# A sliding-window attention followed by a sentence-level mixture of experts: row sums and normalisation in another layout, and the two stages interleaved

**Chip, cores, metric.** One core of a Trainium2 chip. The metric is the device time of one execution in microseconds (us); most executions of a kernel here agree within about 1%.

## The reference

```python
def _attn_ref(q, k, v):                       # (8 batches, 8 heads, 576, 64)
    scores = q @ k.T / sqrt(64)               # per batch and head
    mask = (rel >= 0) & (rel < 64)            # causal, window 64
    attn = softmax(where(mask, scores, -1e9))
    return attn @ v

def _moe_ref(x, w_gate, w1, w2):              # x: (8, 576, 512)
    logits = x.mean(axis=1) @ w_gate          # one expert per batch ("sentence")
    e = argmax(logits); g = softmax(logits)[e]
    return g * (relu(x @ w1[e]) @ w2[e])      # w1[e]: 512 x 1024, w2[e]: 1024 x 512
```

A batch's expert depends on the mean of its whole attention output, so its weights (4 MB of fp32) can be asked for only when its attention is done. Nothing in one batch depends on another.

## The kernel before

It has three stages one after the other: attention of all batches, one gate for all, the MLP of all batches. Attention works on a head pair of a batch at a time (32 pairs), with queries along the free dimension. The row sums come from a second set of matmuls with a matrix of ones, so each sum lies 64 times, once per output row, and the reciprocal runs over all 576 columns:

```python
def stage_b(prev):
    avp = ps_a.tile([128, 1024], FP32, tag="avp")
    lbp = ps_a.tile([128, 1024], FP32, tag="lbp")
    for (j, qlo, qhi, st, sp) in segs:
        for (lhs, op) in ((pvt, avp), (None, lbp)):      # V, then ones
            for hh in range(2):
                ...                                      # 64x64 tiles of the array
    nc.scalar.copy(out=avs, in_=avp[:, 0:S])
    nc.scalar.copy(out=lbs, in_=lbp[:, 0:S])
    nc.vector.reciprocal(out=rl, in_=lbs)                # 128 x 576, L128
    nc.vector.tensor_tensor_reduce(out=xT[:, pbb, php, :], in0=avs, in1=rl, ...)
...
for bb in range(B):                                      # the MLP, after everything
    ...                                                  # load w1t, w2t of the batch's expert
    for ft in range(8):
        php = ps_h.tile([128, 2, 512], FP32, tag="php")  # two banks, bufs=2
        ...                                              # 8 matmuls of 288 columns, relu
    for mt in range(NST):
        ...                                              # 8 matmuls of 512 columns, copy, DMA out
```

The softmax here doesn't subtract the row's maximum and nothing guards it: scores larger than these inputs give would overflow.

## Time and profile before

| | before |
|---|---|
| time, median of 15 runs | 359.7 us (357.2 to 360.9) |
| attention, up to the start of the gate | about 204 us |
| gate and wait for the first expert weights | about 12 us |
| MLP of eight batches, TensorE without a gap | 136 us |
| VectorE's reciprocals | 32 x 3.75 = 119.9 us |

In the lines below, PE is TensorE, PEld its weight loads, DVE is VectorE, ACT is ScalarE, POOL is GpSimd and SPq the queue of SyncE. "Busy" of an engine is the time in which it works on an instruction. "PEclk" is TensorE's granted clock as a share of full speed. In a group line the two numbers after the bar are the group's total busy time and the mean of one instruction in ns, and after the next bar comes the engine's idle time just before, with what ended it. The "pitch" of matmuls is the time from the start of one to the start of the next. The lines of the kernel before are in the prediction.

### The profile page before, as it was taken

Reading aid. Unit: us, or ns where it says so; the run is one execution under the profiler, and the core shown is the slowest. Engines: PE = TensorE matmul, PEld = TensorE weight load, DVE = VectorE, ACT = ScalarE, POOL = GpSimd, SP = SyncE. Lnnn points to the kernel's source line nnn. Section 1 sums busy time; section 2 is a strip of 40 time slices with the busy share of each in tenths; the row PEclk is TensorE's granted clock in tenths of the full one; section 3 lists DMA queues with packets and bytes.
Section 4 is the critical chain, followed back from the end, with each engine's and each line's share of the span. In section 5 each row is a group of like instructions: output and inputs, shape, how many; then the busy total and the mean of one; then the engine's idle time right before and its main releaser. Section 6 shows DMA issues by size and latency. Waiting matters only on the chain.

```text
span 356.7 us, 7472 instructions
## 1 busy us (share of the span) xinstructions
PE 281.1 (79%) x3018; PEld 194.7 (55%) x3018; DVE 189.8 (53%) x179; ACT 185.1 (52%) x356; POOL 130.9 (37%) x189
## 2 busy tenths in 40 slices
PE   0587687778787777787884207999999999999995
PEld 0365565656565665665674205565747474756562
DVE  0049997888887978888879910212130303030312
ACT  2578867676867676767676103342415060605140
POOL 9978665656565656566500030000000011000000
PEclk9999855655655556556556556999999999999999
DMA  9999999999999999999700049999999999998303
GB/s 119 172 153 153 139 125 91 116 96 118 96 118 92 116 99 116 99 112 100 70 3 2 0 77 198 209 266 175 226 164 238 162 229 182 197 221 145 132 29 105
DMA packets 141234, 46.91 MB, mean 132 GB/s; under 512 B 124304, under 2 KB 132496, under 8 KB 141200
## 3 DMA queue, kind: packets, MB, share of 16 engines
q0 software_dynamic: 96416, 27.26, 78.4%
q1 hardware_dynamic: 44784, 19.18, 22.3%
q8 instruction: 24, 0.39, 0.5%
q14 instruction: 10, 0.08, 0.1%
HBM read 63.95 MB, written 9.44 MB: 206 GB/s over the span
## 4 chain that ended last, share of the span: by engine, by line
PE 69%; ACT 17%; issue 5%; DVE 4%; DMA 4%; POOL 1%; POOLq 0%; ACTq 0%; DVEq 0%
PE pso L257 20%; PE php L245 19%; PE tp L171 9%; ACT pt L101 8%; PE lbp L116 8%; PE sps L94 7%; PE avp L116 5%; ACT qT L175 5%; DMA w1t<-in_moe_w_dram 2%; DVE rl L128 2%; ACT kT L175 2%; PE tp L176 2%; DMA qn<-in_q_dram 2%; ACT qT L180 1%; DVE xT L129 1%
## 5 line engine op out<-in xcount | busy, mean ns | idle before, releaser
L128 DVE RECIPROCAL rl<-lbs 128x576 f32<-128x576 f32 x32 | 119.9, 3750 | 24.3 <-ACT lbs L127 24.3
L249 ACT ACTIVATE hT<-php,gwb 128x576 f16<-128x576 f32 x64 | 47.4, 740 | 90.2 <-PE php L245 90.2
L261 DVE COPY ob<-pso 128x512 f32<-128x512 f32 (+1 forms) x40 | 27.6, 689 | 117.3 <-PE pso L257 103.4
L245 PE MATMUL php<-xT,w1t 128*128 128x288 f16 x512 | 66.6, 290 | 8.3 <-DMA w1t<-in_moe_w_dram 8.3
L257 PE MATMUL pso<-w2t,hT 128*128 128x512 f16 (+1 forms) x320 | 71.3, 380 | 0.0
L116 PE MATMUL avp<-pt,vt 64*64 64x128 f16 (+1 forms) x640 | 68.5, 272 | 1.4 <-DVE pt L103 1.4
L116 PE MATMUL lbp<-pt,ones 64*64 64x128 f16 (+1 forms) x640 | 68.7, 271 | 0.0
L116 PEld LDWEIGHTS <-vt 64*64 64x64 f16 x640 | 53.0, 147 | 24.9 <-issue 20.2
L245 PEld LDWEIGHTS <-w1t 128*128 128x128 f16 x512 | 50.0, 99 | 25.4 <-issue 11.2
L156 POOL DMA_DIRECT2D qn<-in_q_dram x63 | 55.0, 876 | 23.5 <-PE tp L176 22.5
L156 POOL DMA_DIRECT2D kn<-in_k_dram x63 | 54.8, 872 | 18.2 <-PE tp L176 17.4
L116 PEld LDWEIGHTS <-ones 64*64 64x64 f16 x640 | 54.6, 150 | 7.6 <-issue 5.7
L257 PEld LDWEIGHTS <-hT 128*128 128x128 f16 (+1 forms) x320 | 31.4, 100 | 37.2 <-issue 3.4
L238 POOL DMA_DIRECT2D w1t<-in_moe_w_dram x8 | 6.0, 756 | 78.1 <-PE php L245 50.5
L101 ACT ACTIVATE pt<-sps 128x1024 f16<-128x1024 f32 x32 | 33.5, 1045 | 0.8 <-PE sps L94 0.8
L94 PEld LDWEIGHTS <-kT 64*64 64x64 bf16 x576 | 27.1, 151 | 9.8 <-issue 9.3
L103 DVE TENSOR_TENSOR pt<-pt,bandm 128x1152 f16<-128x1152 f16 x32 | 22.4, 701 | 18.7 <-ACT pt L102 18.7
L94 PE MATMUL sps<-qT,kT 64*64 64x128 bf16 x512 | 32.2, 289 | 0.0
L126 ACT COPY avs<-avp 128x576 f32<-128x576 f32 x32 | 20.5, 642 | 21.7 <-PE lbp L116 21.1
L171 PE MATMUL tp<-ident,kn 128*128 128x128 bf16 x128 | 16.9, 276 | 15.0 <-ACT qT L180 14.8
L175 ACT CAST kT<-tp 128x512 bf16<-128x512 f32 x32 | 18.8, 588 | 16.4 <-PE tp L171 16.4
L171 PE MATMUL tp<-ident,qn 128*128 128x128 bf16 x128 | 18.6, 297 | 9.8 <-DMA qn<-in_q_dram 9.8
(49 smaller groups left out, 188.2 us busy)
## 6 DMA issues: line engine op xcount, KB each, us to landing
vn<-in_v_dram SPq DMA_DIRECT2D x64, 144.0 KB, 3.3
w1t<-in_moe_w_dram POOLq DMA_DIRECT2D x8, 1024.0 KB, 10.1
w2t<-in_moe_w_dram POOLq DMA_DIRECT2D x8, 1024.0 KB, 10.3
out_dram<-ob SPq DMA_DIRECT2D x32, 256.0 KB, 5.9
qn<-in_q_dram POOLq DMA_DIRECT2D x63, 80.0 KB, 3.6
kn<-in_k_dram POOLq DMA_DIRECT2D x63, 80.0 KB, 3.3
out_dram<-ob SPq DMA_DIRECT2D x8, 128.0 KB, 6.2
bandm<-bandm SPq DMA_DIRECT2D x1, 256.0 KB, 4.6
```

What stands on the lines that cost most here:

```text
L94: nc.tensor.matmul(out=sdst[p0:p0 + 64, :], lhsT=pkT[p0:p0 + 64, ts(j, 64)], rhs=pqT[p0:p0 + 64, j * 64:j * 64 + 128], start=True, stop=Tr ...
L101: nc.scalar.activation(out=pt[:, 0:8, :], in_=sps, func=AF.Exp, scale=scale)
L103: nc.vector.tensor_tensor(out=pt, in0=pt, in1=bandm, op=ALU.mult)
L116: nc.tensor.matmul(out=op[p0:p0 + 64, qlo:qhi], lhsT=lh, rhs=ppt[p0:p0 + 64, j, qlo - 64 * j:qhi - 64 * j], start=st, stop=sp, tile_positi ...
L128: nc.vector.reciprocal(out=rl, in_=lbs)
L156: nc.gpsimd.dma_start(out=tl[:, :, hh, :], in_=tf[hidx:hidx + 640].rearrange("(st p) d -> p st d", p=128))
L171: nc.tensor.matmul(out=tp[:, ts(st, 128)], lhsT=tl[:, st].rearrange("p h d -> p (h d)"), rhs=ident, start=True, stop=True)
L175: nc.scalar.copy(out=dst[:, 0:512], in_=tp)
L245: nc.tensor.matmul(out=php[:, sc, 0:SC], lhsT=w1t[:, kb, ts(ft, 128)], rhs=xT[:, bb, kb, ts(sc, SC)], start=(kb == 0), stop=(kb == 3))
L249: nc.scalar.activation(out=hT[:, ft].rearrange("p (sc s) -> p sc s", sc=2), in_=php[:, :, 0:SC], func=AF.Relu, scale=gwb[:, bb:bb + 1])
L257: nc.tensor.matmul(out=pso[0:n], lhsT=hT[:, fb, mt * 128:mt * 128 + n], rhs=w2t[:, fb, :], start=(fb == 0), stop=(fb == 7))
L261: nc.vector.tensor_copy(out=ob[0:n], in_=pso[0:n])
```

## The change

Its intent: make the reciprocal small, take attention's waits off TensorE by running the MLP of batch b-2 beside the attention of batch b, and move Q and K in larger rows. The diff replaces most of the kernel; its core:

```diff
-            nc.scalar.copy(out=avs, in_=avp[:, 0:S])
-            nc.scalar.copy(out=lbs, in_=lbp[:, 0:S])
-            nc.vector.reciprocal(out=rl, in_=lbs)
-            nc.vector.tensor_tensor_reduce(out=xT[:, pbb, php, :], in0=avs, in1=rl, ...)
+    def st_s(u):        # scores of one slot (128 queries, 8 heads): matmuls, exp, mask product
+    def st_a(u):        # product with [V | 1]; queries on the partitions
+        for h in range(H):
+            for jj in range(nj):
+                nc.tensor.matmul(out=av[64*jj:64*jj+64, h//4, c:c+D+1],
+                    lhsT=pt[:, h%2, h//2, jj, :], rhs=vx[:, 1-jj, i, h, :], ...)
+        nc.vector.reciprocal(out=rl[0:n], in_=avv[0:n, :, :, D:D + 1])        # 8 elements
+        for a in range(2):
+            nc.vector.tensor_tensor(out=x[0:n, a], in0=avv[0:n, a, :, 0:D],
+                                    in1=rl[0:n, a].broadcast_to([n, 4, D]), op=ALU.mult)
+    def st_x(u):        # transpose x back, copy it, row sums for the gate
+    def cast_v(b):      # V to fp16: one copy on VectorE, two (shifted by 64 rows) on GpSimd
+    def gate(b):        # one batch's expert, and its weight DMAs
+    def moe_chunks(b):  # 16 chunks of 4 relu matmuls (one bank, ps_m bufs=2), then 5 of 8
... (loads of Q and K as 2 KB source rows, transposes through PSUM, masks)
+        for s in range(NSLOT + 4):                     # 40 slots, five a batch
+            if i == 1 and 2 <= b:
+                chunks += list(moe_chunks(b - 2))
+            budget = 16.6 / NU if s < NSLOT else 1.0
+            done -= budget if s else 0.0
+            if not chunks:
+                done = 0.0
+            st_s(s);      fill(0.25)                   # fill: MLP chunks while done < part*budget
+            st_a(s - 1);  fill(0.5)
+            tr_main(...); fill(0.75)                   # Q, K transposes of the next batch
+            st_x(s - 2);  fill(1.0)
+        ...                                            # the rest of the MLP
```

## The prediction

> **What bounds the kernel now.** I read the strip of 40 slices first, to see the stages, then the table by stretch, the groups by shape, the chain in order of time, and the timeline of two short stretches of TensorE.
>
> ```profile
> PE   0587687778787777787884207999999999999995
> DVE  0049997888887978888879910212130303030312
> PEclk9999855655655556556556556999999999999999
> GB/s 119 172 153 153 139 125 91 116 96 118 96 118 92 116 99 116 99 112 100 70 3 2 0 77 198 209 266 175 226 164 238 162 229 182 197 221 145 132 29 105
> ```
>
> A slice is 8.9 us. There are three stages: attention (to about 204 us), a hole of about 12 us for gate and first expert weights, and the expert MLP (216 to 352 us). In attention TensorE is never full, VectorE nearly is, and the granted clock is a little over half. In the MLP TensorE is full at full clock and VectorE idles. The table by stretch (time, length, busy time of PE, PEld, DVE, ACT, POOL with counts, clock, DMA share, GB/s) says it in numbers:
>
> ```profile
> 140.00:160.00 20.00, 15.82 (x225) 12.26 (x224) 17.28 (x14) 14.03 (x31) 12.54 (x17) 0.54 1.07 111
> 260.00:280.00 20.00, 20.00 (x120) 11.52 (x119) 4.14 (x6) 6.47 (x9) 2.39 (x3) 1.00 1.01 184
> ```
>
> The chain that ended last is, from 216 us on, TensorE alone. Columns: start, length, what.
>
> ```profile
> 208.42 7.85 DMA w1t<-in_moe_w_dram
> 216.36 9.83 PE php L245 x64
> 226.19 8.75 PE pso L257 x40
> 234.94 8.04 PE php L245 x64
> 242.98 8.75 PE pso L257 x40
> ```
>
> One batch of MLP is 8.04 + 8.75 = 16.8 us of TensorE; eight are 134 us. The groups give the unit costs:
>
> ```profile
> L128 DVE RECIPROCAL rl<-lbs 128x576 f32<-128x576 f32 x32 | 119.9, 3750 | 24.3 <-ACT lbs L127 24.3
> L101 ACT ACTIVATE pt<-sps 128x1024 f16<-128x1024 f32 x32 | 33.5, 1045 | 0.8 <-PE sps L94 0.8
> L103 DVE TENSOR_TENSOR pt<-pt,bandm 128x1152 f16<-128x1152 f16 x32 | 22.4, 701 | 18.7 <-ACT pt L102 18.7
> L261 DVE COPY ob<-pso 128x512 f32<-128x512 f32 x32 | 22.1, 691 | 100.0 <-PE pso L257 100.0
> L175 ACT CAST qT<-tp 128x512 bf16<-128x512 f32 x32 | 19.1, 598 | 3.1 <-PE tp L171 3.1
> ```
>
> The reciprocal alone is 3.75 us per head pair; with the mask product (0.70) and the normalising product (0.74) VectorE needs 5.2 of the some 6 us that a pair takes. So attention is set by VectorE, with transposes and copies waiting for one another beside it.
>
> **What the Trainium skill says.** (1) "TensorE: Matmul & The Clock Gate", Part 1: the array runs at half clock unless it was busy in the last windows. The trace agrees, 0.54 in attention and 1.00 in the MLP. (2) "VectorE: DVE Perf Modes", Walkthrough: a reciprocal is an iterative divide with a repeat count of 8, so it costs per element. The trace has 3750/576 = 6.5 ns per element. (3) "TensorEngine Tiling (Array Packing)", Key Properties: changing the tiling mode drains the array. The timeline shows what this costs (start, length, tile and count):
>
> ```profile
> 31.10 0.63 PE L94 MATMUL sps<-qT,kT 64*64 64x128 bf16 x15
> 31.66 0.40 PE L171 MATMUL tp<-ident,qn 128*128 128x128 bf16 x4
> ...
> 59.87 1.06 PE L94 MATMUL sps<-qT,kT 64*64 64x128 bf16 x16
> 60.73 0.31 PE L94 MATMUL tp<-qT,kT 64*64 64x128 bf16 x2
> ```
>
> At full clock 15 tiled matmuls start (0.63 - 0.22)/14 = 29 ns apart, so the last is issued by 31.53, and the other mode starts at 31.66: a change costs about 0.12 us. At half clock the pitch is 0.86/16 = 54 ns. (4) "SBUF — State Buffer", Who interferes with whom: a VectorE instruction with two SBUF inputs contends with a GpSimd instruction that reads SBUF. In this trace GpSimd issues DMAs and memsets only, so nothing shows it yet.
>
> **The change, part by part.** It rewrites both stages and joins them.
>
> *Removed.* The sums come out of the product with V (a column of ones beside V) and lie one per query and head, so the reciprocal has 8 elements instead of 576: 40 times about 0.2 us (estimate: 8 x 6.5 ns and a fixed part as in the 0.15 us of the gate's 8x1 reciprocal) instead of 120 us. The 640 matmuls with ones, the copies of both accumulators to SBUF (41 us of ACT) and the hole of 12 us go too. Q and K come as 1 KB rows instead of 128 B ones.
>
> *Added.* Transposes of the attention output (160), GpSimd copies of V (two a batch), a row sum over x, and a product per half of the output. In all TensorE has 2760 matmuls instead of 3018.
>
> *Moved.* Attention is cut into 40 slots (5 a batch), and from slot 11 each slot carries 3.32 units of the MLP two batches earlier (its list costs a batch at 16.49 units, so 3.32 x 16.8/16.49 = 3.4 us). Everything is ordered by hand; TensorE takes it in that order.
>
> TensorE in one slot at full clock (estimates from the pitches above; means over the five slots): scores 14.4 matmuls of 64 columns at about 35 ns = 0.5; product with V 14.4 at 35 = 0.5; transposes of Q and K 14.4 of 128 columns at 50 = 0.7; 4 transposes of x at the 63 ns of the old ones = 0.25; six mode changes at 0.12 = 0.7. Sum 2.7 us, with the MLP 6.1.
>
> VectorE in such a slot: mask product of 1024 at 0.63, reciprocal 0.2, two products of 256 out of PSUM 0.8, row sum of 512 0.6, the relus 1.6 x 0.42, the output scaling 0.69, V cast and gate 0.5: 4.1 us. ScalarE: exp 1.05, 1.6 copies of 0.6 for Q and K, the copy of x 0.6, relus 0.65: 3.3. Both are below 6.1, so TensorE is the bound, with short waits because all queues are in order and each accumulator has one or two buffers. I allow 5%.
>
> The sum: (a) to the first slot 17 us (the first matmul came after 9.8 us before; then four groups of transposes at half clock); (b) slots 0 to 10 without MLP: at half clock about 14.4 x 54 ns twice, 1.0 for transposes, 0.43, four changes at 0.2, so 3.8 us each, 42 us; (c) 29 slots at 6.1 plus 5% = 186; (d) three or four draining slots, 3; (e) the MLP left: 8 x 16.49 - 29 x 3.32 = 35.6 units = 36.3 us; (f) the last output, 4 us as now. Total 288 us.
>
> **The rivals.** *A: small matmuls do not overlap.* If neither pairs of column tiles nor weight loads hide, scores and products with V cost 55 to 60 ns, transposes 80, and a slot 3.9 us of attention. Against it: the old tiles do overlap (29 ns). That adds 1.2 x 29 + 8 = 43 us: 330. *B: waits replace VectorE's bound.* The relu of a slot stands behind exp on ScalarE and behind the mask product on VectorE; the GpSimd copies of V (2560 and 2048 elements, two to five us) may hold the mask product up. By my order of a slot an MLP accumulator comes free just when TensorE asks for it, so 0.5 to 1 us more a slot is possible: 305 to 315. *C: DMA becomes the bound.* About 45 MB land, at 288 us 156 GB/s, while the busiest slice now shows 266 GB/s; and weights are asked for four slots (24 us) ahead and landed in about 10 us. I expect them hidden. If not, 310. *D: better than reckoned.* Full clock from slot 0 and fewer waits take off 10 + 9 us and more: 265.
>
> **Range and chances.** Centre 288, from the sum; D and a cheap mode change give 266, B and part of A give 320. Even A leaves the kernel faster than now, since attention at 194 us is mostly waiting and the hole disappears; only several at once reach 353. Faster 0.96, within 2% 0.02, slower 0.02.
>
> **What would show it.** Right: the strip shows TensorE at 8 to 9 from about a fifth of the span on; the clock is 1.0 there, lower before it; the reciprocal falls from 119.9 us to under 12; MLP matmuls keep 127 and 219 ns a piece; a mixed slot takes 6 to 6.5 us; waits of TensorE for DMA of weights do not appear; the end is some 36 us of pure MLP. Wrong: a mixed slot above 7 us with TensorE busy (A), TensorE idle for relus or masks (B), waits on weights (C), or a clock of half in the mixed slots, which would cost most.

## The result, and the profile after

| | before | after |
|---|---|---|
| time, median | 359.7 us (15 runs) | 277.3 us (9 runs, 275.7 to 278.8) |
| ratio | | 0.771 (0.769 to 0.773) |
| TensorE busy | 281.1 us, 79% | 224.4 us, 82% |
| VectorE's reciprocals | 119.9 us | 8.9 us |
| average granted clock (stretches without a record count as full) | 0.78 | 0.955 |

A ratio here is the mean time of one kernel's fast runs over that of the other's of the same rounds, so not quite the ratio of the medians quoted. A run more than 1.5% above the fastest of the same kernel is called slow; all runs of this comparison were fast.

The strip of 40 slices (one slice is 6.9 us):

```profile
PE   0625267758999899969997999699988999899992
DVE  2086487875579757974689468766797688534332
PEclk9999999556999999979999999979999999999999
GB/s 155 199 217 203 96 190 170 114 209 204 213 130 221 181 208 157 223 232 201 161 185 223 197 169 208 220 122 2 90 232 159 2 106 232 169 211 193 49 65 109
```

TensorE is nearly full from slice 10 on. The hole is gone, and half clock is recorded from 49 to 66 us (the first MLP matmul starts at 63.2), and after that only in two stretches of 3.4 us and at the very end. VectorE's load is spread over the whole span. The table by stretch, columns as in the prediction:

```profile
100.00:120.00 20.00, 18.21 (x263) 10.92 (x262) 15.24 (x36) 9.46 (x20) 9.36 (x10) 1.00 1.08 200
235.00:275.00 40.00, 33.63 (x198) 18.67 (x198) 14.70 (x31) 5.72 (x15) 1.48 (x2) 0.99 0.53 132
```

Groups by shape:

```profile
L302 PE MATMUL ph<-xT,w1t 128*128 128x288 f16 x512 | 78.9, 297 | 7.8 <-ACT hT L307 4.9 <-DMA w1t<-in_moe_w_dram 1.3 <-DVE ob L321 0.2
L200 DVE TENSOR_TENSOR pt<-pt,mask 128x1024 f16<-128x1024 f16 x32 | 30.4, 951 | 13.5 <-ACT pt L197 13.3
L229 DVE RECIPROCAL rl<-av 128x8 f32<-128x8 f32 x32 | 6.2, 194 | 2.8 <-PE av L222 2.7
```

The chain that ended last, some of its longest pieces (start, length, what):

```profile
4.02 13.76 DMA v<-in_v_dram
17.93 2.31 POOL vx L137
...
24.39 4.55 DMA tail<-in_k_dram
...
50.48 12.71 DMA w1t<-in_moe_w_dram
...
242.70 8.77 PE po L317 x40
261.33 8.77 PE po L317 x40
```

The start is set in the main by loads (V, then GpSimd's copies of V, then the last rows of Q and K, then the first weights), the end by TensorE. The timeline, from the start and from a slot with MLP work:

```profile
24.00 1.04 PE L152 MATMUL tp<-ident,qk 128*64 128x128 f16 x16
...
77.52 0.64 PE L152 MATMUL tp<-ident,qk 128*64 128x128 f16 x16
...
80.15 0.41 PE L190 MATMUL sp<-qT,kT 64*128 64x64 f16 x16
80.48 0.45 PE L222 MATMUL av<-vx,pt 128*64 128x65 f16 x16
...
81.62 1.89 POOL L138 CAST vx<-v 64x2048 f16<-64x2048 f32 x1
81.71 2.34 DVE L200 TENSOR_TENSOR pt<-pt,mask 128x1024 f16<-128x1024 f16 x1 [0.57 <-ACT pt L197]
```

Three things are to be seen. The same 16 transposes take 1.04 us at 24 us and 0.64 us at 77 us, so the array ran at half clock at the start, although the strip prints a 9 there: the trace's first clock record comes at 45.7 us, and before it the row of the strip means nothing. At full clock 16 scores take only 0.41 us: less one matmul's length of 0.19 us that is (0.41 - 0.19)/15 = 15 ns apiece. The single starts show a pattern: the two matmuls of a pair, on the two row tiles, start 3 or 4 ns apart, and the next pair follows 25 or 26 ns later. And the mask product, about 0.69 us alone, takes 2.34 us here: it ends 0.54 us after GpSimd's copy ends.

Start of each slot's scores, from the trace: slot 0 at 13.4 us, slot 11 at 61.3, then 73.6, 80.1, 85.6, 88.3, 90.5 (slot 16), and slot 39 at 227.5. A batch's five slots are thus very unequal: 12.3, 6.5, 5.5, 2.7, 2.2 us. The account (`done` in the code, in units of which a batch's MLP costs 16.49) is one budget of 3.32 in debt when a batch's chunks arrive (it is cleared before them only if there were none, then `done -= budget` runs), so the first slot takes 6.6 units of MLP and the last none.

### The profile page after: what moved, and what is told of

It reads as the page before. It is cut to its first block, busy times and chain, and to the rows that moved or that the text cites. A ratio compares the mean times of both kernels' runs of the same rounds, so it can differ in the third digit from the quotient of the medians.

```text
span 275.0 us, 6814 instructions
## 1 busy us (share of the span) xinstructions
PE 224.4 (82%) x2800; PEld 141.8 (52%) x2800; DVE 178.0 (65%) x430; ACT 120.8 (44%) x233; POOL 99.4 (36%) x127
## 4 chain that ended last, share of the span: by engine, by line
PE 46%; DVE 20%; DMA 14%; ACT 9%; issue 4%; POOL 3%; SPq 1%; POOLq 0%; DVEq 0%; ACTq 0%
PE ph L302 21%; PE po L317 15%; DMA v<-in_v_dram 5%; ACT pt L197 5%; DMA w1t<-in_moe_w_dram 5%; DVE pt L200 4%; DVE vx L136 3%; DVE hT L309 3%; PE tp L152 3%; DVE ob L321 3%; PE av L222 3%; DMA tail<-in_k_dram 2%; DMA out_dram<-ob 2%; DVE x L233 2%; PE xps L245 2%
## 5 line engine op out<-in xcount | busy, mean ns | idle before, releaser
L302 PE MATMUL ph<-xT,w1t 128*128 128x288 f16 x512 | 78.9, 297 | 7.8 <-ACT hT L307 4.9
L317 PE MATMUL po<-w2t,hT 128*128 128x512 f16 (+1 forms) x320 | 74.7, 380 | 0.0
L309 DVE TENSOR_SCALAR hT<-ph 128x288 f16<-128x288 f32 x64 | 29.0, 454 | 29.3 <-PE ph L302 29.3
L307 ACT ACTIVATE hT<-ph 128x288 f16<-128x288 f32 x64 | 26.4, 413 | 48.2 <-PE ph L302 47.9
L152 PE MATMUL tp<-ident,qk 128*64 128x128 f16 x512 | 25.6, 255 | 17.1 <-POOL ident masks.py:199 7.7
L200 DVE TENSOR_TENSOR pt<-pt,mask 128x1024 f16<-128x1024 f16 x32 | 30.4, 951 | 13.5 <-ACT pt L197 13.3
L197 ACT ACTIVATE pt<-sp 128x1024 f16<-128x1024 f32 x32 | 33.2, 1039 | 9.0 <-PE sp L190 8.9
L321 DVE TENSOR_SCALAR ob<-po,gw 128x512 f32<-128x512 f32 (+1 forms) x40 | 29.7, 742 | 10.9 <-PE po L317 10.8
L152 PEld LDWEIGHTS <-qk 128*64 128x64 f16 x512 | 20.5, 132 | 23.5 <-issue 16.7
L249 DVE TENSOR_REDUCE pp<-xT 128x4 f32<-128x512 f16 (+1 forms) x40 | 25.0, 624 | 11.0 <-ACT xT L248 11.0
L233 DVE TENSOR_TENSOR x<-av,rl 128x256 f16<-128x256 f32 (+1 forms) x80 | 30.1, 417 | 1.4
L248 ACT COPY xT<-xps 128x512 f16<-128x512 f16 (+1 forms) x40 | 22.3, 558 | 11.6 <-PE xps L245 11.5
L79 POOL DMA_DIRECT2D tail<-in_k_dram x32 | 18.7, 587 | 19.4 <-DMA w2t<-in_moe_w_dram 15.1
```

What stands on the lines that cost most here:

```text
L152: nc.tensor.transpose(out=tp[64 * hh:64 * hh + 64, t].rearrange("p a b -> p (a b)"), in_=qks[b][:, 2 * hp + hh, t, :], identity=ident)
L197: nc.scalar.activation(out=pt.rearrange("p a h j x -> p a (h j x)"), in_=sp, func=AF.Exp, scale=scale)
L200: nc.vector.tensor_tensor(out=pt.rearrange("p a h j x -> p (a h j x)"), in0=pt.rearrange("p a h j x -> p (a h j x)"), in1=m.rearrange("p e ...
L233: nc.vector.tensor_tensor(out=x[0:n, a], in0=avv[0:n, a, :, 0:D], in1=rl[0:n, a].broadcast_to([n, 4, D]), op=ALU.mult)
L248: nc.scalar.copy(out=dst, in_=tp[:, :, 0:n])
L249: nc.vector.reduce_sum(out=pps[b][:, :, i], in_=dst, axis=AX.X)
```

## The experiments

Twelve kernels ran, in four groups, each group on one chip and timed against the kernel before in the same rounds. "After" is 277.3 us, ratio 0.771. One execution each of one_fill, even_budget and even_tail was slow and is left out of the ratios. Every run but before_norecip gave right results.

**1. before_norecip.** Is the old attention really paced by the reciprocal?

```diff
-            nc.vector.reciprocal(out=rl, in_=lbs)
+            nc.vector.tensor_copy(out=rl, in_=lbs)      # wrong numbers on purpose
```

> The kernel before with its 576-element reciprocal replaced by a copy of the same tile (wrong numbers on purpose). Theory (VectorE's reciprocal sets the pace of the old attention): VectorE then needs about 0.7 + 0.7 + 0.6 us per head pair instead of 5.2, and the pair takes what TensorE at half clock and ScalarE need, about 4.3 to 5 us instead of 6.1; 320 to 335 us instead of 360. Rival (the old attention is a chain of transposes and copies, the reciprocal is hidden beside it): 350 us or more.

Measured: 301.3 us, ratio 0.839. Its table by stretch, to be held against the line 140:160 in the prediction:

```profile
100.00:120.00 20.00, 15.08 (x337) 11.69 (x338) 9.61 (x19) 19.74 (x45) 17.25 (x26) 1.00 1.91 153
```

VectorE falls from 17.3 to 9.6 us in 20, ScalarE rises from 14.0 to 19.7 and is the new bound, and TensorE does 337 matmuls instead of 225. The clock is 1.00 instead of 0.54. The theory holds, and by more than I expected (58 us, not 25 to 40). I had left TensorE at half clock, and here it kept the full one; that this makes up the difference is likely, but no run separates it.

**2. wide_recip.** The reverse: the changed kernel with a big reciprocal put back.

```diff
-        nc.vector.reciprocal(out=rl[0:n], in_=avv[0:n, :, :, D:D + 1])
+        for a in range(2):      # 256 elements each
+            nc.vector.reciprocal(out=rl[0:n, a], in_=avv[0:n, a, :, D:D + 1].broadcast_to([n, 4, D]))
```

(Cut: `rl` is 64 times as large, and the products read it without a broadcast.)

> The changed kernel with the reciprocal of each sum taken 64 times, 512 elements a slot in two instructions of 256, instead of 8 (right result, the same values). Theory (the reciprocal set the pace before, and would in the new design): VectorE gets some 3.3 us more a slot, 5.8 in slots without MLP and 7.5 with it, so it becomes the bound and the join gives little: 335 to 355 us. Rival (the join hides it, VectorE had 35% free): below 300 us.

Measured: 362.1 us, ratio 1.005. Two lines, of its groups and of its list of waits (who waited for whom, total us, times, longest):

```profile
L230 DVE RECIPROCAL rl<-av 128x256 f32<-128x256 f32 x64 | 107.4, 1716 | 3.6 <-PE av L222 3.5
...
PE av L222 <- DVE x L234: 49.1, 20, 4.1
```

With reciprocals of about the old size the whole rewrite, join and all, is worth nothing: VectorE is busy 283.6 us and TensorE waits 49 us for its products. The size is not quite the old one: with the smaller slots (26.8 us) the reciprocals take 134 us, before 120. It came out above the expected 335 to 355; the direction is the theory's.

**3. unjoined, 4. unjoined_four.** What is the join worth? The MLP of all batches goes after all attention, with xT, gate indices and gate weights kept for eight batches and weights loaded two batches ahead. unjoined_four also lets the relu matmuls rotate over four PSUM banks.

```diff
-            if i == 1 and 2 <= b:
-                chunks += list(moe_chunks(b - 2))
...
+        for b in range(B):
+            for _, f in moe_chunks(b):
+                f()
+            if b + 2 < B:
+                load_w(b + 2)
```

> The changed kernel with the whole expert MLP after all attention instead of beside it (right result). Theory (the join is worth what attention leaves idle on TensorE): attention alone takes about 14 + 40 x 3.7 = 160 us at half clock, with the MLP of 134 us and the ends about 305 us, so the new attention gives some 50 of the 82 us and the join some 30. Rival (the join is everything): 330 us or more. Rival (the join gives nothing, since TensorE is the bound in both): 285 us or less.

> unjoined with the relu matmuls of the MLP rotating over four accumulators, two of them in banks that attention has left (right result). Theory (the unjoined MLP lost about 14 us to two accumulators, as its mean pitch of 154 ns over some 500 relu matmuls against 122 shows): about 312 us, so that the join without this handicap is worth some 35 us. Rival (the MLP waits for something else): above 320 us.

Measured: unjoined 325.8 us (0.909), unjoined_four 314.0 us (0.873). Of unjoined, the table by stretch and a piece of its chain:

```profile
120.00:140.00 20.00, 15.18 (x298) 12.33 (x294) 15.79 (x43) 14.34 (x27) 7.89 (x4) 0.50 0.47 79
```

```profile
189.67 0.67 PE ph L308 x4
190.87 0.67 PE ph L308 x4
192.07 0.67 PE ph L308 x4
```

Slots 0 to 39 start 3.73 us apart ((159.0 - 13.6)/39), as reckoned; the clock is recorded from 112 us on, full for 6.8 us and then half until 170. But I had taken the MLP at the old 16.8 us a batch, and it takes 18.7, 15 us more in all: a pair of chunks takes 1.20 us (the starts in the chain) instead of 8 x 0.122 = 0.98. Every pair waits for one of two accumulators to be emptied. With four, the mean pitch of the relu matmuls falls from 154 to 129 ns (from 235 us on) and the time by 12 us, as the second expectation said. So the join is worth 325.8 - 277.3 = 48 us with the accumulators equal, and 37 against unjoined_four. Of my rivals for unjoined none fits. The forecast of 305 us was 21 too low: 15 for the reason just given, and the MLP began at 166.9 us, not at 160. Alone, the new attention is no faster than the old one without its reciprocal: unjoined_four is 314 us, before_norecip 301.

**5. v_by_dma.** GpSimd's copies replaced by a VectorE cast and two DMAs within SBUF.

```diff
-        nc.gpsimd.tensor_copy(out=t[64:128, 1, :, :, 0:D], in_=s[0:64])
-        nc.gpsimd.tensor_copy(out=t[0:64, 1, 1:5, :, 0:D], in_=s[64:128, 0:4])
+        nc.vector.tensor_copy(out=t[0:64, 0, 4, :, 0:D], in_=s[0:64, 4])
+        nc.sync.dma_start(out=t[64:128, 1], in_=t[0:64, 0])
+        nc.sync.dma_start(out=t[0:64, 1, 1:5], in_=t[64:128, 0, 0:4])
```

> The changed kernel with the two GpSimd copies of V per batch replaced by a VectorE cast of 512 elements more and two SBUF-to-SBUF DMAs (right result). Theory (GpSimd's copies hold up VectorE's mask product, 951 ns in the mean against 690 ns where it runs alone, and TensorE waits for it): the mask product falls to about 700 ns in the mean and the time by 4 to 8 us, to some 271 us. Rival (the delay of the mask product is hidden, since the product with V comes a slot later): mask product falls, time within 2 us of 277.

Measured: 285.7 us (0.793), 8 us longer. A line of its groups, and one of its chain:

```profile
L201 DVE TENSOR_TENSOR pt<-pt,mask 128x1024 f16<-128x1024 f16 x32 | 22.1, 692 | 15.0 <-ACT pt L198 14.7
```

```profile
54.80 19.32 DMA vx<-vx
```

The contention is shown: without GpSimd's copies the mask product takes 692 ns instead of 951. But a new wait took its place: one copy took 19.3 us from issue to landing (TensorE waited 18.3 us in all for such copies). The copies stand behind V's 256 B rows in one DMA queue, and that queue hardly moved: from 55 to 64 us it brought 0.14 MB, while the other queue, with the first expert weights, brought 1.71 MB. What the contention costs is not told by this run.

**6. v_on_act.** The same copies on ScalarE, a slot later.

```diff
+                if i == 4:
+                    cast_v2(b + 1)      # the two copies, with nc.scalar.copy
```

> The changed kernel with the two copies of V per batch on ScalarE, one slot later, instead of on GpSimd (right result). Theory (the copies on GpSimd cost VectorE, as the run with DMAs showed by a mask product of 692 ns, and TensorE waits for some of it): mask product about 695 ns, no new wait, since ScalarE has 56% of its time free, 3 to 6 us off, 272 us. Rival (hidden, or given back where exp and relu stand behind 4.2 us of copies on ScalarE): 275 to 281 us.

Measured: 294.0 us (0.820), worse than either expectation. The mask product is again 692 ns, but the copies (2.33 and 1.90 us, as long as on GpSimd) stand ahead of ScalarE's other work: the row sum waits 35.6 us in all for ScalarE's copy of x (11.0 after), TensorE 17.4 us. A free share of 56% says nothing about a queue taken in order. Of the three places tried for the copies in every batch GpSimd is the best, contention and all.

**7. three_acc.** Three MLP accumulators, one transpose buffer.

```diff
-    ps_t = ... bufs=2 ...   ps_m = ... bufs=2
+    ps_t = ... bufs=1 ...   ps_m = ... bufs=3
```

> The changed kernel with three MLP accumulators instead of two and one buffer instead of two for the transposes (right result). Theory (two accumulators make TensorE wait: the mean start-to-start time of the relu matmuls is 154 ns where back to back is 122): the mean falls to 122 to 130 ns, 10 to 14 us off, less 3 to 6 us of new waits where transposes share one buffer, 268 to 271 us. Rival (the transposes' single buffer costs more than the third accumulator gives): 280 us or more.

Measured: 289.7 us (0.809). From 67 us to the end the relu matmuls' mean pitch is 135 ns (156 in the changed kernel), so the third buffer does what it should, but TensorE's transposes of x wait 27.7 us for ScalarE's copy of K out of the one buffer. The rival holds.

**8. one_fill.** A slot's MLP in one piece instead of four.

```diff
-            fill(0.25) ... fill(0.5) ... fill(0.75)
             fill(1.0)
```

> The changed kernel with the MLP's share of a slot in one piece at its end instead of in four pieces (right result). Theory (mode changes of about 0.1 us each are a cost that the order could save): three changes a slot less in some 23 slots, 7 us off, 270 us. Rival (the pieces are there to give ScalarE and VectorE time to empty the two accumulators, and TensorE waits without them): 3 to 10 us longer than 277, with more waits of the relu matmuls for the relus.

Measured: 288.9 us (0.802). The rival holds, if not quite in its place: the relu matmuls' mean pitch is no worse (156 ns in both from 67 us on), while the step from a batch's last relu chunk to its first output chunk, which needs that relu, takes 1.6 us six times (9.8 us); in the changed kernel attention stands between them.

**9. start_order.** Masks and last rows of Q and K first.

```diff
-        cast_v(0)
-        load_tail(0)
+        ...                 # the 33 mask instructions, moved here
+        load_tail(0)
+        cast_v(0)
```

> The changed kernel with the masks built before V is cast and the Q and K tails of the first two batches loaded before GpSimd copies V (right result). Theory (the start is a chain that the whole kernel waits for: the trace has TensorE waiting 4.2 us for the tails in slot 3, and the mask copies stretched by GpSimd's copies until 22.4 us): 5 to 7 us off, 271 us. Rival (V lands at 17.8 us and the expert weights at 63 us, and these set the start): 1 us or less.

Measured: 277.1 us (0.772). Nothing: GpSimd's copies of V now come after its 16 tail loads, so the wait moved to slot 1 (20.5 to 29.1 us, before 20.1 to 25.0). The rival's number is right, its reason (V's landing) only in part, as run 12 shows.

**10. even_budget.** The debt removed.

```diff
+                fresh = not chunks                 # before the batch's chunks are added
-            if not chunks:
+            if not chunks or fresh:
                 done = 0.0
```

> The changed kernel with the slot account set to zero where a batch's MLP begins (right result). In the trace the first slot of each batch takes about 12 us and the last, without MLP, 2 to 3, because the account starts one budget in debt. Theory (the empty slots leave TensorE waiting for attention's chain): with about 3.3 units in each of five slots the waits of the empty slots go, 3 to 6 us off, about 272 us. Rival (the same work and the same waits, only elsewhere): within 2 us of 277.

Measured: 272.3 us (0.756), as the theory has it. Slots 11 to 16 start at 64.1, 70.8, 76.9, 83.5, 87.9, 91.1: 27 us a batch instead of 29.2. The intervals of the two ratios (0.748 to 0.763, and 0.769 to 0.773) do not overlap.

**11. even_tail.** even_budget, and four accumulators once attention has ended.

```diff
+            if tail and (ft * 2 + sc) % 4 >= 2:    # every other pair of chunks
+                pool, tag = ((ps_s, "s"), (ps_a, "a"))[sc]
+                ph = pool.tile([128, 2, 512], FP32, tag=tag, name="ph")[:, 0]
```

> The changed kernel with the account of even_budget, and after the last attention slot the relu matmuls rotate over four accumulators, two of them in the PSUM banks that attention has left (right result). Theory (two accumulators cost TensorE a wait in each pair of chunks, 154 ns a matmul in the mean against 122 back to back): in the tail's about 105 relu matmuls this is 3.4 us, so about 269 us and a mean pitch of 122 to 125 ns in the tail. Rival (the wait is for something else, such as weight loads): within 1 us of even_budget's 272.

Measured: 268.9 us (0.747), as expected; from 230 us on the mean pitch falls from 151 to 126 ns. The intervals of the ratios just overlap (0.744 to 0.750, and 0.748 to 0.763 for even_budget), but the traces agree: from the start of slot 39 to the end it is 50.5 us instead of 53.7.

**12. even_tail_start.** even_tail with the start freed: the order of start_order, and the first batch's two copies of V on ScalarE.

```diff
+        load_tail(0)
+        cast_v(0, nc.scalar.copy)
```

> even_tail with the masks built first, the tails of Q and K loaded before V is cast, and the first batch's two copies of V on ScalarE, which then waits for V anyway (right result). Theory (start_order gained nothing because GpSimd's copies of V then came after its 16 tail loads; with both freed of each other the chain shortens): slot 11 begins 3 to 5 us sooner and the time falls by as much from even_tail's 269, to about 265 us. Rival (V's landing at some 18 us sets the start, whoever copies it): 268 to 270 us.

Measured: 264.2 us, ratio 0.734 (0.730 to 0.738). Slot 11 starts at 58.7 us instead of even_tail's 62.1. This is the fastest version, 4.7% shorter than the changed kernel (0.734/0.771). Its strip:

```profile
PE   0434767679999899989998999899999896999992
PEclk9999999999999999999999999999999998999999
```

## Why the prediction was right

288 us was forecast, with 266 and 320 as its ends, and 277.3 measured. Its sum, against the trace (span 275.0 us):

| term | predicted us | measured us |
|---|---|---|
| (a) to the first slot | 17 | 13.4 |
| (b) slots 0 to 10 | 42 | 47.9 |
| (c) slots 11 to 38, at 6.1 and 5% | 179 | 166.2 |
| (c, d, e) slot 39 to the last matmul | 6.4 + 3 + 36.3 | 42.6 |
| (f) the last output | 4 | 4.9 |

The number owes something to luck: (b) was 6 us too low and (c) 13 us too high, and inside (c) errors of both signs met. What was right in the mechanism, and what was not:

- *The bound of the old attention.* Right, and shown from both sides: 301 us without the reciprocal, 362 us with it in the new kernel. What the prediction missed is its size, and that TensorE, waiting behind it, also ran at half clock (0.54, and 1.00 without the reciprocal).
- *The MLP keeps its pace.* Only half right. The output matmuls keep 216 ns. The relu matmuls' mean pitch went from the 127 ns forecast to 156 (154 in the tail), because the change gave them two banks where the old kernel had four. I counted the buffers and expected "short waits"; unjoined_four and even_tail show the wait and its cure.
- *TensorE in a mixed slot.* The mis-sized terms of (c). Attention's matmuls were put at 1.95 us a slot; the start-to-start times over slots 11 to 38 sum to 0.94 us a slot (scores 15 ns each instead of 35, product with V 19, transposes 28 instead of 50). The waits were put at 5%, 0.3 us; the stretched relu matmuls alone come to 337 x (156.3 - 122) ns = 11.6 us, 0.4 us a slot, and the waits for mask and normalisation add to that. The two errors partly cancelled. A mode change costs 0.10 us (218 against 122 ns where a relu matmul is followed by another mode), near the 0.12 read from the old trace.
- *The account.* The even 3.4 us of MLP in every slot, on which (c) rests, did not exist: 6.6 units, then three times 3.3, then none. The code showed it, and I did not follow the account through the first slot of a batch. even_budget puts its price at 5 us. The sum of (c) does not show it, since the slots of a batch together carry the same MLP.
- *Slots 0 to 10.* Half clock was right (1.04 us for 16 transposes), but the pace was set by waits for loads and GpSimd that the prediction took as hidden: 4.4 us in the mean, not 3.8. Run 12 takes some of it back.
- *Rivals.* A (no overlap of small matmuls) is wrong. B is the one that is there: waits for accumulators, and GpSimd's hold on the mask product, whose cost in time no run separates. C is not: TensorE waited 1.3 us for expert weights, once.
- *The join.* Worth 48 us; the rest of the rewrite, without it, brings 34 us (359.7 to 325.8). What of these 34 us the larger rows of Q and K bring, no run separates. The parts do not add: with a large reciprocal they give nothing together. What pays is VectorE off the bound first, and then TensorE's dense matmuls filling attention's waits. That the MLP's matmuls also keep the clock full for attention fits the 0.50 of unjoined against 1.00 here; how much of the 48 us that is, no run separates.

## What to carry to other kernels

Before joining two stages, ask which engine would be the bound of the joined one: here an oversized instruction on VectorE would have eaten the whole gain. Lay a statistic out so that it exists once per row before it is inverted. In an order written by hand, follow the account of the filler through its first slot, count the accumulators of the filler as if it ran alone, and judge a free engine by what stands in its queue, not by its free share.

## What the Trainium skill lacked or had wrong

- "TensorE: Matmul & The Clock Gate", Part 1, "Wait — 56ns, not 53.3ns?": it says that matmuls never start less than about 25 ns apart, however small. For tiled ones that holds only from pair to pair: the 64-column scores on two row tiles start 3 or 4 ns apart within a pair and 25 or 26 ns after it, 15 ns in the mean. The page's own Part 3 has the 4 ns for tiles; the two passages are to be read together. The products with V on two column tiles have a mean of 19 ns. Missing this was half of the error in (c).
- The same page, Part 4: it says that the full clock does not engage for transposes. Where MLP matmuls run around them, they have it: 16 transposes took 0.64 us, 28 ns apiece, against 1.04 us where the array was at half clock. Whether transposes alone would bring the full clock, no run here shows.
- "TensorEngine Tiling (Array Packing)", Key Properties: it names the drain at a mode change but not its cost. 0.10 us here.
- "VectorE: DVE Perf Modes", Walkthrough: it gives a repeat count of 8 for the reciprocal and no time. Read as 8 cycles an element it would be 8.3 ns at the page's 0.96 GHz (an estimate); measured are 6.5 ns (3750/576).
- "DMA: Bandwidth & Descriptors" gives no time that a copy may wait behind other transfers: here a copy within SBUF landed after 19.3 us, behind V's rows in its own queue and beside the expert weights in the other.
